# Three phases per batch in place of two, in a windowed-attention and gated-MLP kernel

## The chip, the cores and the metric

The kernel runs on one core of a Trainium2 chip. The metric is the device time of one execution in microseconds (us), the median of several runs. The "span" of a profile is the time from first to last instruction of the one profiled execution; it is about 1.7 to 2 us shorter than the timed value. Engines: PE is TensorE's matmul, PEld its weight load, DVE is VectorE, ACT is ScalarE, POOL is GpSimd, SP issues the output transfers.

## The reference, cut to what matters

Eight batches. Each has windowed attention (8 heads, 576 positions, width 64: four heads with a plain window of 32, four with a window dilated by 4), and then a gated MLP with a mixing matrix over the positions.

```python
scores = q @ k.T / sqrt(64)                  # masked by window, per head
attn   = softmax(scores);  x = concat_heads(attn @ v)        # (576, 512)
h = gelu_tanh(x @ w_in);  u, v = split(h)                    # (576, 512) each
v_n = (v - mean(v)) / sqrt(var(v) + 1e-6) * g_ln
v_s = w_sg @ v_n + b_sg                                      # over positions
out = x + (u * v_s) @ w_out
```

## The kernel before

The program is a list of small work items, each of which issues instructions to several engines. `merge` interleaves up to three lists. Every engine then works through its own instructions in the order of issue, so the interleaving fixes each engine's queue. The items of one batch `b`:

```python
a_T(b, g)    # transposes of q, k of a head pair: PE -> PSUM; copies qT, kT by ACT, half of kT by DVE (L223)
a_S(b, h)    # scores of a head: PE; exp by ACT; mask by DVE, or by POOL where h % 4 == 3
a_AV(b, g)   # value sums of a head pair: PE; DVE: reciprocal rc, then
             #     onorm = poa * rc        (L272, the eviction)
a_X(b, g)    # transpose of onorm: PE (pxt, L288); copy to xT by ACT (L291, or L295 and L297)
m_zv(b, i)   # v half of x @ w_in: PE (pz, L312); gelu by ACT (vv, L316); statistics st, mv by DVE (L321);
             #     rs = (var + 1e-6) ** -0.5 by POOL
m_vn(b, i)   # normalised v: DVE (vn, L331)
m_zu(b, ph)  # u half: PE (pu, L341); gelu by ACT
m_sgu(b, ph) # w_sg product: PE (pv, L354); DVE: vs = pv*g + b (L358), gat = u * vs (L361)
m_out(b, i)  # output product: PE (po, L371, L374); copy osb by ACT (L377); output by SP
```

PSUM has room for four of the tiles (`bufs=4`), taken in turn. The interleaving and the two phases of a period `p`:

```python
def merge(*lists):                      # every item of a list weighs the same
    items = [((i + 0.5) / len(x), n, i, f) for n, x in enumerate(lists)
             for i, f in enumerate(x)]
    for _, _, _, (f, *a) in sorted(items, key=lambda t: t[:3]):
        f(*a)

for p in range(B + 2):
    # first phase: T and S of batch p, beside sgu and out of batch p-2   (prep_wsg at p == 1)
    att = [T0, T1, S0, S1, T2, S2, S3, T3, S4, S5, S6, S7, cp_vd]       # (shortened)
    mlp = [sgu 0..3, out 0..2]                                          # (shortened)
    merge(att, mlp, io)
    # second phase: AV and X of batch p, beside zv, vn, zu of batch p-1
    att = [AV0, AV1, X0, AV2, X1, AV3, X2, X3]                          # (shortened)
    mlp = [zv0, zv1, vn0, zv2, vn1, zu0, vn2, zu1, zu2, zu3]            # (shortened)
    io  = [plain q, k of batch p+2; dilated q, k of batch p+2]          # (shortened)
    merge(att, mlp, io)
```

The softmax here doesn't subtract the row's maximum and nothing guards it: scores larger than these inputs give would overflow.

Of the kernel before, what the change touches and what calls it, by code (L numbers as in the profile page):

```python
# [11 lines left out]
FP16 = mybir.dt.float16  # L12
# [3 lines left out]
B, H, S, D = 8, 8, 576, 64  # L16
# [11 lines left out]
HS = S // 2  # L28
# [25 lines left out]
def kernel(  # L54
# [12 lines left out]
    nc = tc.nc  # L67
# [6 lines left out]
    sb = ctx.enter_context(tc.tile_pool(name="sb", bufs=2))  # L74
# [3 lines left out]
    def psum(name):  # L78
        return ps.tile([128, 2, 512], FP32, tag="ps", name=name)
# [25 lines left out]
    def setup_consts():  # L105
        nc.sync.dma_start(ident16, IDT.ap())
        nc.sync.dma_start(masks, MSK.ap())
        nc.vector.memset(mhalf, -0.5)
        for i in range(NKT):
            for hd in range(2):  # L110
                nc.vector.memset(kTs[i][hd], 0.0)
            nc.vector.memset(kIs[i], 0.0)
        for t in vps + vds:
            nc.vector.memset(t[0:HALO], 0.0)
            nc.vector.memset(t[:, :, :, 64:65], 1.0)
        for t in PTb:
            nc.vector.memset(t[:, S:PTW], 1.0)
        nc.vector.memset(wsgT16[0:64, 4, :], 0.0)


    def dma(dst, src):
        nc.gpsimd.dma_start(dst, src)  # L122
# [3 lines left out]
    def open_batch(b):  # L126
        qp = ld.tile([QB, NB, 4, D], FP16, tag="qp", name="qp")
        kp = ld.tile([QB, NB, 4, D], FP16, tag="kp", name="kp")
        qd = ld.tile([TB, 4, 2, 4, D], FP16, tag="qd", name="qd")
        kd = ld.tile([TB, 4, 2, 4, D], FP16, tag="kd", name="kd")  # L130
        loaded[b] = ((qp, kp), (qd, kd))

    def ld_plain(b, h0):
        if h0 == 0:
            open_batch(b)
        for t, src in zip(loaded[b][0], (q, k)):
            for h in range(h0, h0 + 2):
                dma(t[:, :, h, :], src[b][h].rearrange("(a p) d -> p a d", p=QB))

    def ld_dil(b):  # L140
        for t, src in zip(loaded[b][1], (q, k)):
            dma(t.rearrange("p h f r d -> p (h f) (r d)"),
                src[b][4:8].rearrange("h (f p r) d -> p (h f) (r d)", p=TB, r=4))

    def ld_vp(b, h0, n):
        vp = vps[b % NV]
        x = v[b][h0:h0 + n].rearrange("h (a p) d -> p (h a) d", p=QB)
        y = vp[:, h0:h0 + n].rearrange("p h a d -> p (h a) d")
        dma(y[HALO:KB, :, 0:D], x)
        dma(y[0:HALO, 1:, 0:D], x[QB - HALO:QB, 0:n * NB - 1])  # L150
# [3 lines left out]
    def ld_vd(b):  # L154
        vm = ld.tile([KB, 4, 4, D], FP16, tag="vm", name="vm")
        vt = ld.tile([KB, 4, 3, D], FP16, tag="vt", name="vt")
        x = v[b][4:8].rearrange("h (m r) d -> m h (r d)", r=4)
        dma(vm.rearrange("p h r d -> p h (r d)"), x[0:KB])
        for r in range(2):
            dma(vt[r:KB:2].rearrange("p h r d -> p h (r d)"),  # L160
                x[NM - 64:NM, :, D * r:D * r + 3 * D])
        vraw[b] = (vm, vt)
# [7 lines left out]
    def ld_win():  # L170
        dma(w_in16, moe_w_in.rearrange("(g p) f -> p g f", p=128))
# [25 lines left out]
    def a_T(b, g):  # L197
        plain, dil = loaded[b]
        pq, pk = psum("pq"), psum("pk")
        for t, pt in zip(plain if g < 2 else dil, (pq, pk)):  # L200
            if g < 2:
                for a in range(NB):
                    nc.tensor.matmul(pt[:, a // 3, QB * (a % 3):QB * (a % 3) + QB],
                                     t[:, a, 2 * g:2 * g + 2, :], ident16[0:QB, 0:QB],
                                     start=True, stop=True)
            else:
                for hd in range(2):
                    for c in range(4):
                        j, f = divmod(c, 2)
                        nc.tensor.matmul(pt[:, hd, TB * c:TB * c + TB],  # L210
                                         t[:, 2 * g - 4 + hd, f, 2 * j:2 * j + 2, :],
                                         ident16[0:TB, 0:TB], start=True, stop=True)
        qT = sb.tile([128, 2, HS], FP16, tag="qT", name="qT", bufs=3)
        nc.scalar.copy(qT, pq[:, :, 0:HS])  # L214
        if g < 2:
            kT = kTs[(2 * b + g) % NKT]
            k0, k1 = (kT[hd][64 * hd:64 * hd + 64, HALO:].rearrange(
                "p (j w) -> p j w", j=2) for hd in range(2))
        else:
            kT = kIs[(2 * b + g) % NKT]  # L220
            k0, k1 = (kT[64 * r:64 * r + 64, :, :, r] for r in range(2))
        nc.scalar.copy(k0, pk[0:64, :, 0:HS])
        nc.vector.tensor_copy(k1, pk[64:128, :, 0:HS])  # L223
        qkT[b, g] = (qT, kT)

    def a_S(b, h):
        qT, kT = qkT[b, h // 2]
        pss = psum("pss")
        if h < 4:
            kx, qx = kT[h % 2], qT.rearrange("p j w -> p (j w)")  # L230
            for a in range(NB):
                nc.tensor.matmul(pss[:, a // 3, QB * (a % 3):QB * (a % 3) + QB],
                                 kx[:, QB * a:QB * a + KB], qx[:, QB * a:QB * a + QB],
                                 start=True, stop=True)
        else:
            for j in range(2):
                kx = kT[:, h % 2, NM * j:NM * j + NM, :]
                qx = qT[:, h % 2, NM * j:NM * j + NM]
                for r in range(2):
                    nc.tensor.matmul(pss[:, j, 128 * r:128 * r + 128],  # L240
                                     kx[:, 0:KB, r], qx[:, 0:128], start=True, stop=True)
                nc.tensor.matmul(pss[:, j, 256:HS], kx[:, NM - 64:NM, :],
                                 qx[:, 128:NM].unsqueeze(1).broadcast_to([128, 2, 16]),
                                 start=True, stop=True)
        PT = PTb[(8 * b + h) % NPT]
        nc.scalar.activation(PT[:, 0:S].rearrange("p (j w) -> p j w", j=2),  # L246
                             pss[:, :, 0:HS], AF.Exp, scale=0.125)
        eng = nc.gpsimd if h % 4 == 3 else nc.vector
        eng.tensor_tensor(PT[:, 0:S], PT[:, 0:S], masks[:, h // 4], AO.mult)
        PTs[b, h] = PT  # L250

# [128 lines left out]
            nc.sync.dma_start(out[b][MT[ti] + lo:MT[ti] + 128, :], osb[lo:128, c, :])  # L380


    def merge(*lists):

        items = [((i + 0.5) / len(x), n, i, f) for n, x in enumerate(lists)
                 for i, f in enumerate(x)]
        for _, _, _, (f, *a) in sorted(items, key=lambda t: t[:3]):
            f(*a)

    setup_consts()  # L390
    for h0 in (0, 2):
        ld_plain(0, h0)
    ld_vp(0, 0, 4)
    ld_dil(0)
    ld_vd(0)
    ld_win()
    for p in range(B + 2):
        att, mlp, io = [], [], []
        if p < B:
            att = [(a_T, p, 0), (a_T, p, 1), (a_S, p, 0), (a_S, p, 1),  # L400
                   (a_T, p, 2), (a_S, p, 2), (a_S, p, 3),
                   (a_T, p, 3), (a_S, p, 4), (a_S, p, 5),
                   (a_S, p, 6), (a_S, p, 7), (cp_vd, p)]
        if p == 1:
            mlp = [(prep_wsg, i) for i in range(5)]
        if p >= 2:
            mlp = ([(m_sgu, p - 2, ph) for ph in range(4)] +
                   [(m_out, p - 2, i) for i in range(3)])
        if p + 1 < B:
            if p == 0:  # L410
                io = [(ld_plain, 1, 0), (ld_plain, 1, 2), (ld_dil, 1)]
            io += [(ld_vp, p + 1, 0, 4), (ld_vd, p + 1)]
        if p == 0:
            io += [(ld_wsg,)]
        if p == 1:
            io += [(ld_wout,)]
        merge(att, mlp, io)
        att, mlp, io = [], [], []
        if p < B:
            att = [(a_AV, p, 0), (a_AV, p, 1), (a_X, p, 0), (a_AV, p, 2), (a_X, p, 1),  # L420
                   (a_AV, p, 3), (a_X, p, 2), (a_X, p, 3)]
        if 1 <= p <= B:
            mlp = [(m_zv, p - 1, 0), (m_zv, p - 1, 1), (m_vn, p - 1, 0), (m_zv, p - 1, 2),
                   (m_vn, p - 1, 1), (m_zu, p - 1, 0), (m_vn, p - 1, 2)]
            mlp += [(m_zu, p - 1, ph) for ph in range(1, 4)]
        if p + 2 < B:
            io = [(ld_plain, p + 2, 0), (ld_plain, p + 2, 2), (ld_dil, p + 2)]
        merge(att, mlp, io)


# [28 lines left out]
```

## Time and profile before

| | before |
|---|---|
| time, median of the first 3 runs | 318.75 us |
| span of the profiled execution | 316.6 us |
| time from one batch's first pz to the next one's, undisturbed | 34.9 us |
| first pv (the fill) | 71.1 us |
| from the seventh batch's first pv to the end (the drain) | 37.2 us |

The profile page's first part (busy time and share of the span, by engine), and the first line of its fourth part (the chain of work that ended last, by engine):

```profile
PE 233.4 (74%) x2494; PEld 164.5 (52%) x2494; DVE 200.2 (63%) x378; ACT 185.3 (59%) x270; POOL 140.7 (44%) x191
...
DVE 35%; PE 29%; POOL 13%; ACT 10%; DMA 7%; issue 5%; POOLq 0%; DVEq 0%; ACTq 0%
```

No engine is near full, and the chain hops between all of them. The windows view splits one period into its two phases (second phase first). Columns: the stretch, its length, then busy time of PE, PEld, DVE, ACT and POOL with counts of instructions, the granted PE clock (1.00 is full speed), the time of the DMA packets as a share of the 16 DMA engines' time (above 1 where packets overlap), and GB/s:

```profile
123.70:141.00 17.30, 12.42 (x138) 8.34 (x136) 13.08 (x26) 10.89 (x17) 11.29 (x16) 1.00 0.57 68
141.00:158.60 17.60, 15.04 (x173) 10.88 (x173) 11.01 (x17) 12.47 (x20) 6.13 (x8) 1.00 1.03 119
```

In the first row PE works 12.4 of 17.3 us. The waits view says what it waits for (who waits and for what, with lines; then us in total, times, longest):

```profile
PE pxt L288 <- DVE onorm L272: 32.3, 23, 1.9
...
DVE st L321 <- ACT vv L316: 16.0, 8, 7.9
...
PE po L371 <- DVE gat L361: 8.6, 8, 1.1
```

The timeline of one second phase shows where the largest of these comes from. The brackets at the end of a line give the idle time before it and what ended it:

```profile
158.48 1.89 PE L312 MATMUL pz<-w_in_71,xT 128*128 128x512 f16 x8
...
165.01 0.43 PE L288 MATMUL pxt<-ident_69,onorm 96*128 96x96 f16 x6 [1.87 <-DVE onorm L272]
...
170.81 0.44 PE L288 MATMUL pxt<-ident_69,onorm 128*128 128x128 f16 x6 [1.28 <-DVE onorm L272]
...
173.87 0.66 PE L288 MATMUL pxt<-ident_69,onorm 128*128 128x128 f16 x6 [1.64 <-DVE onorm L272]
...
164.00 0.95 DVE L272 TENSOR_TENSOR onorm<-poa,rc 96x768 f16<-96x768 f32 x1
...
172.86 0.96 DVE L272 TENSOR_TENSOR onorm<-poa,rc 128x768 f16<-128x768 f32 x1
```

The phase opens with a zv group (pz at 158.48), and the first onorm starts at 164.00. The last starts at 172.86. Each X waits for its onorm, and PE cannot pass it.

### The profile page before, as it was taken

Reading aid. Unit: us, or ns where it says so; the run is one execution under the profiler, and the core shown is the slowest. Engines: PE = TensorE matmul, PEld = TensorE weight load, DVE = VectorE, ACT = ScalarE, POOL = GpSimd, SP = SyncE. Lnnn points to the kernel's source line nnn. Section 1 sums busy time; section 2 is a strip of 40 time slices with the busy share of each in tenths; the row PEclk is TensorE's granted clock in tenths of the full one; section 3 lists DMA queues with packets and bytes.
Section 4 is the critical chain, followed back from the end, with each engine's and each line's share of the span. In section 5 each row is a group of like instructions: output and inputs, shape, how many; then the busy total and the mean of one; then the engine's idle time right before and its main releaser. Section 6 shows DMA issues by size and latency. Waiting matters only on the chain.

```text
span 316.6 us, 6153 instructions
## 1 busy us (share of the span) xinstructions
PE 233.4 (74%) x2494; PEld 164.5 (52%) x2494; DVE 200.2 (63%) x378; ACT 185.3 (59%) x270; POOL 140.7 (44%) x191
## 2 busy tenths in 40 slices
PE   0373548868877779768876979768877878788984
PEld 0263445546545656546544756456545755564552
DVE  7533339957669493949478393949488665961760
ACT  1461549558475858477565858467666857533603
POOL 8946958492427741493229541593222011300400
PEclk9999999979999999999999899999999999999999
DMA  9999999699535997099626987099620004002104
GB/s 131 127 202 129 172 134 152 94 76 124 91 118 39 93 90 188 4 76 124 127 83 42 116 66 185 7 75 121 124 85 2 2 2 149 2 0 113 39 0 149
DMA packets 91467, 28.92 MB, mean 91 GB/s; under 512 B 71664, under 2 KB 86064, under 8 KB 91440
## 3 DMA queue, kind: packets, MB, share of 16 engines
q0 software_dynamic: 85232, 18.48, 66.2%
q1 hardware_dynamic: 6208, 10.06, 9.2%
q8 instruction: 19, 0.31, 0.4%
q14 instruction: 8, 0.07, 0.1%
HBM read 37.54 MB, written 9.44 MB: 148 GB/s over the span
## 4 chain that ended last, share of the span: by engine, by line
DVE 35%; PE 29%; POOL 13%; ACT 10%; DMA 7%; issue 5%; POOLq 0%; DVEq 0%; ACTq 0%
PE po L371 10%; DVE st L321 7%; DVE vs L358 6%; DVE onorm L272 5%; DVE gat L361 5%; PE pz L312 4%; DMA w_in_71<-in_moe_w_in_dram 4%; POOL kp L122 3%; PE pv L354 3%; PE po L374 3%; DVE vn L331 3%; DMA wsg_73<-in_moe_w_sg_dram 3%; ACT vv L316 3%; POOL rs L324 3%; POOL qp L122 2%
## 5 line engine op out<-in xcount | busy, mean ns | idle before, releaser
L371 PE MATMUL po<-w_out_72,gat 128*128 128x512 f16 x160 | 42.7, 379 | 8.6 <-DVE gat L361 8.6
L354 PE MATMUL pv<-wsgT_74,vn 128*128 128x288 f16 x320 | 43.9, 286 | 5.4 <-DVE kI_86 L223 1.2
L377 ACT COPY osb<-po 128x1024 f32<-128x1024 f32 (+1 forms) x24 | 21.0, 875 | 36.8 <-PE po L374 29.2
L288 PE MATMUL pxt<-ident_69,onorm 96*128 96x96 f16 (+2 forms) x192 | 15.3, 220 | 32.8 <-DVE onorm L272 32.3
L354 PEld LDWEIGHTS <-vn 128*128 128x128 f16 x320 | 30.8, 97 | 14.6 <-issue 5.6
L312 PE MATMUL pz<-w_in_71,xT 128*128 128x512 f16 x160 | 38.1, 379 | 0.2 <-ACT PT_95 L246 0.2
L341 PE MATMUL pu<-xT,w_in_71 128*128 128x288 f16 x256 | 37.9, 295 | 0.0
L321 DVE BATCH_NORM_STATS2 st<-vv 128x6 f32<-128x512 f32 x40 | 27.0, 675 | 16.0 <-ACT vv L316 16.0
L214 ACT CAST qT<-pq 128x576 f16<-128x576 f32 x32 | 20.5, 641 | 25.9 <-PE pq L210 13.0
L323 POOL TENSOR_SCALAR rs<-mv 128x2 f32<-128x2 f32 (+1 forms) x24 | 6.8, 282 | 59.9 <-DVE mv L322 59.5
L288 PEld LDWEIGHTS <-onorm 96*128 96x128 f16 (+1 forms) x192 | 10.6, 104 | 40.3 <-DVE onorm L272 40.3
L272 DVE TENSOR_TENSOR onorm<-poa,rc 96x768 f16<-96x768 f32 (+1 forms) x32 | 30.6, 956 | 1.1
L295 ACT CAST xT<-pxt 128x512 f16<-128x512 f32 x16 | 20.8, 1300 | 17.3 <-PE pxt L288 17.2
L344 ACT ACTIVATE u<-pu 128x576 f16<-128x576 f32 x32 | 21.9, 683 | 12.4 <-PE pu L341 12.4
L358 DVE SCALAR_TENSOR_TENSOR vs<-pv,g_col,b_bc 128x576 f16<-128x576 f32 x32 | 26.1, 814 | 4.3 <-PE pv L354 3.8
L122 POOL DMA_DIRECT2D kp<-in_k_dram x32 | 23.2, 728 | 9.2 <-DMA w_in_71<-in_moe_w_in_dram 3.9
L341 PEld LDWEIGHTS <-w_in_71 128*128 128x128 f16 x256 | 23.9, 100 | 6.0
L316 ACT ACTIVATE vv<-pz 128x1024 f32<-128x1024 f32 (+1 forms) x24 | 21.0, 881 | 9.0 <-PE pz L312 7.5
L122 POOL DMA_DIRECT2D qp<-in_q_dram x32 | 25.3, 797 | 1.5 <-POOLq L443 0.9
L371 PEld LDWEIGHTS <-gat 128*128 128x128 f16 x160 | 13.5, 97 | 21.4 <-DVE gat L361 13.7
L331 DVE TENSOR_SCALAR vn<-vv,mv,rs 128x512 f16<-128x512 f32 x40 | 21.3, 570 | 2.8 <-POOL rs L324 2.8
L312 PEld LDWEIGHTS <-xT 128*128 128x128 f16 x160 | 14.6, 98 | 14.0 <-issue 0.3
(179 smaller groups left out, 494.2 us busy)
## 6 DMA issues: line engine op xcount, KB each, us to landing
out_dram<-osb SPq DMA_DIRECT2D x32, 256.0 KB, 2.2
qp<-in_q_dram POOLq DMA_DIRECT2D x32, 72.0 KB, 3.0
kp<-in_k_dram POOLq DMA_DIRECT2D x32, 72.0 KB, 3.3
qd<-in_q_dram POOLq DMA_DIRECT2D x8, 288.0 KB, 6.1
kd<-in_k_dram POOLq DMA_DIRECT2D x8, 288.0 KB, 7.1
vm<-in_v_dram POOLq DMA_DIRECT2D x8, 256.0 KB, 4.4
vt<-in_v_dram POOLq DMA_DIRECT2D x16, 96.0 KB, 4.1
vp_87<-in_v_dram POOLq DMA_DIRECT2D x4, 288.0 KB, 8.5
```

Of the source, the lines that this page charges most:

```text
L122: nc.gpsimd.dma_start(dst, src)
L272: nc.vector.tensor_tensor(onorm.rearrange("p a h d -> p h a d"), pv[:, :, :, 0:64], rc.unsqueeze(3).broadcast_to([rows, 2, NB, 64]), AO.mult)
L288: nc.tensor.matmul(pxt[:, s // 3, c:c + n], onorm[:, s, :, :], ident16[0:rows, 0:n], start=True, stop=True)
L312: nc.tensor.matmul(pz[:, c, :], xT[:, g4, MT[ti]:MT[ti] + 128], w_in16[:, g4, DH:DFF], start=(g4 == 0), stop=(g4 == 3))
L316: nc.scalar.activation(vv[:, 0:n], pz[:, 0:n], AF.Gelu_apprx_tanh)
L321: nc.vector.bn_stats(st[:, c, :], vv[:, c, :])
L331: nc.vector.tensor_scalar(vn[:, ti, :], vv[:, c, :], mv[:, c, 0:1], rs[:, c, :], AO.subtract, AO.mult)
L341: nc.tensor.matmul(pu[:, j, 0:HS], w_in16[:, g4, 128 * ph:128 * ph + 128], xT[:, g4, HS * j:HS * j + HS], start=(g4 == 0), stop=(g4 == 3))
L344: nc.scalar.activation(us[b][:, ph, :].rearrange("p (j w) -> p j w", j=2), pu[:, :, 0:HS], AF.Gelu_apprx_tanh)
L354: nc.tensor.matmul(pv[:, j, 0:HS], vn[:, kp, 128 * ph:128 * ph + 128], wsgT16[:, kp, HS * j:HS * j + HS], start=(kp == 0), stop=(kp == 4))
L358: nc.vector.scalar_tensor_tensor(vs.rearrange("p (j w) -> p j w", j=2), pv[:, :, 0:HS], g_col[:, ph:ph + 1], b_bc.rearrange("p (j w) -> p ...
L371: nc.tensor.matmul(po[:, c, :], gat[:, ph, ts], w_out16[:, ph, :], start=(ph == 0), stop=False)
```

## The change

Three things: scores beside the gating unit, value sums beside the output product, and the first MLP half beside the next batch's transposes, with the MLP one period closer to its attention. The diff also brings two things: `merge` now weighs each item by an estimated cost, and the start-up is rearranged (w_sg is loaded ahead of batch 1's values, batch 0's dilated q and k ahead of its values, and batch 0's masks all go to VectorE). Besides, qT gets five buffers in place of three.

```diff
-        qT = sb.tile([128, 2, HS], FP16, tag="qT", name="qT", bufs=3)
+        qT = sb.tile([128, 2, HS], FP16, tag="qT", name="qT", bufs=5)
-        eng = nc.gpsimd if h % 4 == 3 else nc.vector
+        eng = nc.gpsimd if b and h % 4 == 3 else nc.vector
+    COST = {a_T: 0.7, a_S: 0.35, a_AV: 0.7, a_X: 0.4, m_zv: 1.5, m_zu: 1.0, m_sgu: 1.25,
+            m_out: 1.9, prep_wsg: 0.35}
     def merge(*lists):
-        items = [((i + 0.5) / len(x), n, i, f) for n, x in enumerate(lists)
-                 for i, f in enumerate(x)]
+        items = []
+        for n, x in enumerate(lists):
+            costs = [COST.get(f[0], 0.02) for f in x]
+            at = 0.0
+            for i, (f, c) in enumerate(zip(x, costs)):
+                items.append(((at + c / 2) / sum(costs), n, i, f))
+                at += c
...
-    for p in range(B + 2):
+    merge(T(0, range(4)))
+    for p in range(B + 1):
         # first phase
+            att = [(a_S, p, h) for h in range(8)] + [(cp_vd, p)]
+            mlp = [(m_sgu, p - 1, ph) for ph in range(4)]
+            io = [(ld_plain, 1, 0), (ld_plain, 1, 2), (ld_dil, 1), (ld_wsg,)]     # p == 0
         # second phase
             att = [AV0, AV1, X0, AV2, X1, AV3, X2, X3]                            # (shortened)
+            mlp = [(m_out, p - 1, i) for i in range(3)]
+            io = [(ld_vp, 1, 0, 4), (ld_vd, 1), (ld_wout,)]                       # p == 0
         # third phase
+            att = T(p + 1, range(4))
+            mlp = [zv0, zv1, vn0, zv2, vn1, zu0, vn2, zu1, zu2, zu3 of batch p]   # (shortened)
+            io = [(prep_wsg, i) for i in range(5)]                                # p == 0
```

More of the change, by code (lines that the diff above doesn't have):

```diff
@@ L380, in m_out, with T @@
             nc.sync.dma_start(out[b][MT[ti] + lo:MT[ti] + 128, :], osb[lo:128, c, :])
+    COST = {a_T: 0.7, a_S: 0.35, a_AV: 0.7, a_X: 0.4, m_zv: 1.5, m_zu: 1.0, m_sgu: 1.25,
+            m_out: 1.9, prep_wsg: 0.35}
     def merge(*lists):
-        items = [((i + 0.5) / len(x), n, i, f) for n, x in enumerate(lists)
-                 for i, f in enumerate(x)]
+        items = []
[5 more added lines that the diff above has]
+                at += c
         for _, _, _, (f, *a) in sorted(items, key=lambda t: t[:3]):
             f(*a)
+    def T(b, gs):
+        return [(a_T, b, g) for g in gs] if b < B else []
     setup_consts()
@@ L392 @@
         ld_plain(0, h0)
+    ld_dil(0)
     ld_vp(0, 0, 4)
-    ld_dil(0)
     ld_vd(0)
     ld_win()
-    for p in range(B + 2):
+    merge(T(0, range(4)))
+    for p in range(B + 1):
         att, mlp, io = [], [], []
         if p < B:
-            att = [(a_T, p, 0), (a_T, p, 1), (a_S, p, 0), (a_S, p, 1),
-                   (a_T, p, 2), (a_S, p, 2), (a_S, p, 3),
-                   (a_T, p, 3), (a_S, p, 4), (a_S, p, 5),
-                   (a_S, p, 6), (a_S, p, 7), (cp_vd, p)]
-        if p == 1:
-            mlp = [(prep_wsg, i) for i in range(5)]
-        if p >= 2:
-            mlp = ([(m_sgu, p - 2, ph) for ph in range(4)] +
-                   [(m_out, p - 2, i) for i in range(3)])
-        if p + 1 < B:
-            if p == 0:
-                io = [(ld_plain, 1, 0), (ld_plain, 1, 2), (ld_dil, 1)]
-            io += [(ld_vp, p + 1, 0, 4), (ld_vd, p + 1)]
+            att = [(a_S, p, h) for h in range(8)] + [(cp_vd, p)]
+        if p >= 1:
+            mlp = [(m_sgu, p - 1, ph) for ph in range(4)]
         if p == 0:
-            io += [(ld_wsg,)]
-        if p == 1:
-            io += [(ld_wout,)]
+            io = [(ld_plain, 1, 0), (ld_plain, 1, 2), (ld_dil, 1), (ld_wsg,)]
+        elif p + 1 < B:
+            io = [(ld_plain, p + 1, 0), (ld_plain, p + 1, 2)]
         merge(att, mlp, io)
@@ L421 @@
                    (a_AV, p, 3), (a_X, p, 2), (a_X, p, 3)]
-        if 1 <= p <= B:
-            mlp = [(m_zv, p - 1, 0), (m_zv, p - 1, 1), (m_vn, p - 1, 0), (m_zv, p - 1, 2),
-                   (m_vn, p - 1, 1), (m_zu, p - 1, 0), (m_vn, p - 1, 2)]
-            mlp += [(m_zu, p - 1, ph) for ph in range(1, 4)]
-        if p + 2 < B:
-            io = [(ld_plain, p + 2, 0), (ld_plain, p + 2, 2), (ld_dil, p + 2)]
-        merge(att, mlp, io)
+        if p >= 1:
+            mlp = [(m_out, p - 1, i) for i in range(3)]
+        if p == 0:
+            io = [(ld_vp, 1, 0, 4), (ld_vd, 1), (ld_wout,)]
+        elif p + 1 < B:
+            io = [(ld_dil, p + 1)]
+        merge(att, mlp, io)
+        if p < B:
+            att = T(p + 1, range(4))
+            mlp = [(m_zv, p, 0), (m_zv, p, 1), (m_vn, p, 0), (m_zv, p, 2),
+                   (m_vn, p, 1), (m_zu, p, 0), (m_vn, p, 2)]
+            mlp += [(m_zu, p, ph) for ph in range(1, 4)]
+            io = []
+            if p == 0:
+                io += [(prep_wsg, i) for i in range(5)]
+            elif p + 1 < B:
+                io += [(ld_vp, p + 1, 0, 4), (ld_vd, p + 1)]
+            merge(att, mlp, io)
 _INS = ['q', 'k', 'v', 'moe_w_in', 'moe_g_ln', 'moe_w_sg', 'moe_b_sg', 'moe_w_out']
```

## The prediction

> **What bounds it now.** No single engine. By the windows view one batch takes a period of 34.9 us (the same pz matmul recurs in the chain of waits at 88.8, 123.7, 158.6, 194.7, 229.6, 263.7). A period holds 27.4 us of TensorE, 24.1 of VectorE, 23.4 of ScalarE; the rest is waits inside in-order queues (chain: VectorE 35%, TensorE 29%, GpSimd 13%, ScalarE 10%). In the second phase VectorE is fullest (13.1 of 17.3 us): four onorm evictions (0.96 us) share its queue with five st (0.68) and five vn, and TensorE waits 32 us in all for onorm (waits view). The rs pair on GpSimd sits among ten q/k DMA issues (0.75 us each). Around the periods are a fill of 53 us (DMA about 99% busy in the slices; w_sg lands at 43.6) and a drain from 279.5 to 316.6.
>
> **What the change does.** No arithmetic is removed. It
> 1. removes one stage of depth: the drain step "sgu + out of batch 6" (279.5 to 291, 11.5 us) moves into a full period, batch 0's first MLP half into the fill;
> 2. asks for w_sg before batch 1's values (0.83 MB less ahead of it at 150 GB/s: 5 us earlier, estimate 38), and keeps batch 0's masks off GpSimd, which hold AV until 35 us now;
> 3. spreads GpSimd: rs shares a phase with 5 DMA issues, not 10;
> 4. takes st and vn out of the phase with onorm;
> 5. adds a tight chain: zv directly follows X of the same batch. The last xT copies (1.30 + 0.40 us, twice) come first on ScalarE; estimated 2.5 us of idle TensorE per period. Table loads (1.28 us) go from 13 to 16.
>
> **A period, costed** from timeline durations. Scores + sgu: TensorE 7.1, VectorE about 9.5, ScalarE 5.6. AV + X + out: 8.4, 4.5, 6.2. Transposes + zv + zu: 10.3, 9.8, 10.5. The maxima add to 28.4, against 27.8 for the two phases now: a tie by work alone. Walking the queues by hand (four PSUM tiles, in order) gives 4.5 us from the last AV to zv, 12.6 for phase three, 16.1 for phases one and two: 33.2; with unmodelled gaps I take 34. The steady state gains only about 1 us per batch.
>
> **Sum.** Batch 0's third phase ends at about 52.5 us; six periods of 34 = 204; phases one and two of batch 7, 20.6; zv + zu, 9.5; the last sgu + out, 15.6 as now. 302 us of span, 303 timed. Most of the gain is fill and drain; about 6 us is the period. Break-even is a period near 36.5.
>
> **What the profile would show.** First pz of each batch 33 to 35 us apart; first pv at about 52 (71 now); TensorE waiting about 2 us for xT before each batch's first pz; VectorE light in the AV phase; GpSimd well under 13% of the chain; onorm waits much below 32 us; w_sg landing at 36 to 40.
>
> The Trainium skill's "Perfetto Trace Analysis" (Tensor Engine Instruction) calls ScalarE, VectorE and GpSimd strict FIFO. The trace agrees: ready work stands behind waiting copies (kT casts waiting 10.3 us). So interleaving order, not busy time, decides.
>
> **What would make it wrong.** Phase three limited by PSUM rotation (VectorE frees pk behind st and vn), or phase one by VectorE with the sgu chain exposed: a period over 35.5 removes the 2%. Eight loads issued beside the masks may delay PT 3 and 7. If phases overlap more than I walked, a period of 31 gives 285.

## The result, and the profile after

The time is 307.25 us (median of four runs, 305.54 to 308.69), against 318.97 us for the kernel before in the same rounds. The ratio is 0.9639, with a 95% interval of 0.9582 to 0.9696: faster by 3.6%. The ratios here and below are worked out from runs of the same rounds, so they are not quite the ratios of the medians.

The page's first part and the first line of the chain, after:

```profile
PE 237.3 (78%) x2494; PEld 165.0 (54%) x2494; DVE 196.2 (64%) x380; ACT 188.0 (62%) x272; POOL 139.3 (46%) x189
...
DVE 3%; PE 3%; ACT 1%; POOLq 0%; issue 0%; POOL 0%; DVEq 0%; ACTq 0%
```

The chain cannot be compared: in this trace it could be followed back only from the end to 278 us, so its shares add up to 8% of the span. The windows view of one period, third phase first, then first and second:

```profile
140.44:155.35 14.91, 11.44 (x112) 7.28 (x110) 8.24 (x17) 12.89 (x20) 5.50 (x9) 1.00 0.56 78
155.35:163.37 8.02, 7.36 (x90) 6.09 (x88) 6.54 (x13) 6.25 (x10) 7.40 (x11) 1.00 1.05 94
163.37:175.36 11.99, 10.23 (x114) 6.87 (x112) 8.36 (x15) 4.29 (x6) 4.56 (x5) 0.86 0.95 128
```

The waits view after:

```profile
DVE st L321 <- ACT vv L316: 55.3, 9, 6.7
...
PE po L371 <- DVE gat L361: 12.8, 8, 1.8
...
PE pz L312 <- ACT xT L295: 11.8, 14, 0.9
...
PE pxt L288 <- DVE onorm L272: 2.8, 3, 1.7
```

The wait for onorm is gone (32.3 us to 2.8). In its place PE waits 11.8 us for xT, which it never did before, and 12.8 us instead of 8.6 for gat; and VectorE, which used to be the fullest engine of its phase, now waits 55.3 us for the first vv of each batch. The timeline shows both waits, in two different batches:

```profile
98.11 0.39 PE L371 MATMUL po<-w_out_72,gat 128*128 128x512 f16 x1 [1.76 <-DVE gat L361]
...
98.67 1.91 PE L371 MATMUL po<-w_out_72,gat 128*128 128x512 f16 x4
...
140.44 0.59 PE L312 MATMUL pz<-w_in_71,xT 128*128 128x512 f16 x2
141.83 0.39 PE L312 MATMUL pz<-w_in_71,xT 128*128 128x512 f16 x1 [0.81 <-ACT xT L295]
...
143.11 1.25 PE L312 MATMUL pz<-w_in_71,xT 128*128 128x512 f16 x5 [0.89 <-ACT xT L295]
```

The second line is a group of four matmuls that takes 1.91 us; the same group takes 1.03 us in other batches. That is a drop of the PE clock: the trace's clock records have it at half speed for 3.41 us from 98.4, and again from 166.7 and 235.0 (the third row of the windows above holds the second drop, hence its 0.86). It comes in every second batch, so the period alternates between 33.4 and 34.9 us.

The 14 profiles together show when such a drop comes. In each profile the drops start whole multiples of 3.41 us apart, as on a fixed grid. Cut each profile into stretches of this grid, from 60 us to 8 us before the end and leaving out those already inside a drop: this gives 917 stretches. In 54 of them PE was busy for less than 54% of the time, and 26 of these were followed by a drop; of the other 863 none was. In the kernel after, PE was busy for 1.65 of the 3.41 us before each of its three drops (windows view). In the batch from 122.2 the same wait of 1.76 us (131.26 to 133.02) is split by the grid at 132.5 into stretches with 2.14 and 2.92 us of work, and no drop follows. So in these profiles every drop came behind a thin stretch, but a thin stretch was not enough: half of the 54 had no drop behind them.

**Where the time came from.** The first pv of each batch cuts a span into a fill (up to the first), six full periods, and a drain (from the seventh to the end). These numbers are worked out from the timelines of the profiled executions:

| | fill | mean of six periods | drain | fill + drain |
|---|---|---|---|---|
| before | 71.1 | 34.71 | 37.2 | 108.4 |
| after | 54.5 | 34.08 | 46.8 | 101.2 |

Of the 10.9 us of span, 7.2 come from fill and drain and 6 x 0.63 = 3.8 from the period (rounded). That is close to the prediction's split. The table also shows something the prediction did not expect: the fill is 16.7 us shorter, but the drain is 9.6 us longer. Whether the shallower pipeline itself brings anything is the first question for the experiments.

### The profile page after: what moved, and what is told of

Read it like the earlier page. It is cut to its first block, busy times and chain, and to the rows that moved or that the text cites. A ratio compares the mean times of both kernels' runs of the same rounds, so it can differ in the third digit from the quotient of the medians. Undisturbed runs are those within 1.5% of the kernel's fastest.

```text
span 305.7 us, 6136 instructions
## 1 busy us (share of the span) xinstructions
PE 237.3 (78%) x2494; PEld 165.0 (54%) x2494; DVE 196.2 (64%) x380; ACT 188.0 (62%) x272; POOL 139.3 (46%) x189
## 5 line engine op out<-in xcount | busy, mean ns | idle before, releaser
L321 DVE BATCH_NORM_STATS2 st<-vv 128x6 f32<-128x512 f32 x40 | 27.2, 679 | 55.7 <-ACT vv L316 55.3
L312 PE MATMUL pz<-w_in_71,xT 128*128 128x512 f16 x160 | 44.1, 404 | 18.1 <-ACT xT L295 11.8
L371 PE MATMUL po<-w_out_72,gat 128*128 128x512 f16 x160 | 45.4, 399 | 12.8 <-DVE gat L361 12.8
L354 PE MATMUL pv<-wsgT_74,vn 128*128 128x288 f16 x320 | 45.0, 286 | 6.2 <-DVE vn L331 1.8
L341 PE MATMUL pu<-xT,w_in_71 128*128 128x288 f16 x256 | 35.1, 286 | 3.2 <-ACT u L344 2.6
L354 PEld LDWEIGHTS <-vn 128*128 128x128 f16 x320 | 29.2, 97 | 15.4 <-issue 5.3
L341 PEld LDWEIGHTS <-w_in_71 128*128 128x128 f16 x256 | 24.9, 98 | 11.6 <-issue 4.7
L371 PEld LDWEIGHTS <-gat 128*128 128x128 f16 x160 | 14.4, 102 | 26.7 <-DVE gat L361 17.0
L214 ACT CAST qT<-pq 128x576 f16<-128x576 f32 x32 | 20.3, 634 | 13.1 <-PE pq L203 10.9
L344 ACT ACTIVATE u<-pu 128x576 f16<-128x576 f32 x32 | 20.9, 652 | 8.0 <-PE pu L341 7.9
L122 POOL DMA_DIRECT2D qp<-in_q_dram x32 | 24.2, 766 | 2.2 <-DMA kd<-in_k_dram 0.9
L361 DVE TENSOR_TENSOR gat<-u,vs 128x576 f16<-128x576 f16 x32 | 20.5, 642 | 1.4
L295 ACT CAST xT<-pxt 128x512 f16<-128x512 f32 x16 | 20.6, 1346 | 0.6 <-PE pxt L288 0.6
L324 POOL TENSOR_TENSOR rs<-rs,mhalf 128x2 f32<-128x2 f32 (+1 forms) x24 | 17.5, 729 | 2.0
```

Of the source, the lines that this page charges most:

```text
L122: nc.gpsimd.dma_start(dst, src)
L312: nc.tensor.matmul(pz[:, c, :], xT[:, g4, MT[ti]:MT[ti] + 128], w_in16[:, g4, DH:DFF], start=(g4 == 0), stop=(g4 == 3))
L321: nc.vector.bn_stats(st[:, c, :], vv[:, c, :])
L341: nc.tensor.matmul(pu[:, j, 0:HS], w_in16[:, g4, 128 * ph:128 * ph + 128], xT[:, g4, HS * j:HS * j + HS], start=(g4 == 0), stop=(g4 == 3))
L344: nc.scalar.activation(us[b][:, ph, :].rearrange("p (j w) -> p j w", j=2), pu[:, :, 0:HS], AF.Gelu_apprx_tanh)
L354: nc.tensor.matmul(pv[:, j, 0:HS], vn[:, kp, 128 * ph:128 * ph + 128], wsgT16[:, kp, HS * j:HS * j + HS], start=(kp == 0), stop=(kp == 4))
```

## The experiments

Theory A, the prediction's: the removed drain stage and the earlier start-up bring the fill and drain gain, the three phases bring about 1 us per period. Rival B: the depth is worth little. Rival C: the weights, which the prediction did not mention at all, carry the steady-state gain. Twelve kernels ran; all gave correct results. Period (the mean of the six) and fill + drain of a row below are from its own profile, and the time is a median of four runs beside the kernel before on the same chip (before: 318.9 to 319.8 us). e9, e10 and e11 ran on another chip than the rest.

| run | phases | weights | start-up | time, us | ratio to before | period | fill + drain |
|---|---|---|---|---|---|---|---|
| before | 2 | no | old | 319 | 1 | 34.71 | 108.4 |
| e3 | 2 | no | new | 314.4 | 0.984 | 34.74 | 104.0 |
| e4 | 2 | yes | old | 300.95 | 0.941 | 32.05 | 106.9 |
| e6 | 2 | yes | new | 292.45 | 0.919 | 31.80 | 101.1 |
| e5 | 3 | no | new | 314 | 0.989 | 34.24 | 102.9 |
| e2 | 3 | yes | old | 311.0 | 0.972 | 33.77 | 107.6 |
| after | 3 | yes | new | 307.25 | 0.964 | 34.08 | 101.2 |

### e1_deep3: three phases at the old depth

```diff
-    for p in range(B + 1):
+    for p in range(B + 2):
-            mlp = [(m_sgu, p - 1, ph) ...]      # and m_out, p - 1; m_zv, m_vn, m_zu, p
+            mlp = [(m_sgu, p - 2, ph) ...]      # and m_out, p - 2; m_zv, m_vn, m_zu, p - 1
```

prep_wsg moves to the first phase of p = 1.

> The three phases of the changed kernel, but with the old depth: the MLP of batch p-1 runs beside batch p+1's transposes, its sgu and output one period later. Theory A (my prediction: most of the gain is the removed drain stage, about 11.5 us): the period stays near 34.1 us or falls by the 1.7 us xT wait at most, but a drain stage comes back, so the time is clearly above the changed kernel's 307 us, about 312 to 318. Rival B (depth as such is worth little: the shallow version only moves batch 7's lone attention phases to the end, about 47 us of tail against about 38, and what gained is the fill and the phase grouping): the time is within 1.5% of 307 us, and the first pz no longer waits for xT.

Measured: 304.01 us, ratio 0.951. One period deeper is not slower but about 1% faster than the changed kernel. An undisturbed period is 32.2 us. Theory A asked for 312 us or more and falls; rival B holds. This run alone does not separate the depth from the wait for xT, because the deeper version also loses most of that wait (2.1 us in 5 waits, against 11.8 in 14). The cut by first pv does not fit e1, whose sixth period is short (26.8 us: no transposes of a next batch are left). Over the five periods before it e1 takes 165.7 us and the kernel after 169.5; the rest of the span is 137.4 us in e1 and 136.2 in the kernel after. By this cut the stage of depth is worth about 1 us at the ends, not 11.5; each clock drop, some 1.5 us, blurs it.

### e2_latefill and e3_beforefill: the start-up edits taken away, and alone

```diff
 # e2, on the kernel after                          # e3, on the kernel before: the reverse
-    eng = nc.gpsimd if b and h % 4 == 3 else nc.vector
+    eng = nc.gpsimd if h % 4 == 3 else nc.vector
-    ld_dil(0); ld_vp(0, 0, 4)
+    ld_vp(0, 0, 4); ld_dil(0)
-    io = [plain 1, dil 1, wsg]; second phase: [vp 1, vd 1, wout]
+    io = [plain 1, dil 1, vp 1, vd 1, wsg]; second phase: [wout]
```

> The changed kernel with the old load order (batch 1's values ahead of w_sg, batch 0's values ahead of its dilated q/k) and batch 0's h%4==3 masks back on GpSimd. If the fill is bound by the arrival of w_sg, the first pv moves from 54.5 to about 60 us and the whole time rises by about 5 us, to about 312, with an unchanged period of 34.1 us. If the fill is bound by something else, the time stays within 1% of 307.

> The kernel before with only the start-up edits: w_sg ahead of batch 1's values, dilated q/k ahead of values for batch 0, batch 0's masks all on VectorE. If the start-up edits alone are worth what I put on them (5 us), the time is about 314 us with an unchanged period of 34.9 us; if they are worth more than half of the 11.5 us gain, it is under 313; if nothing, 319.

Measured: 310.98 and 314.39 us. The tile view of pv (first and last start at the end of the line) gives the fill of before, after, e2, e3 and e6, in this order, one fence each:

```profile
L354 PE MATMUL pv<-wsgT_74,vn x320: 282/286/297, 71.1 to 305.3; 128*128 128x288 f16 x160
```

```profile
L354 PE MATMUL pv<-wsgT_74,vn x320: 282/286/297, 54.4 to 294.4; 128*128 128x288 f16 x160
```

```profile
L354 PE MATMUL pv<-wsgT,vn x320: 282/286/448, 59.3 to 299.0; 128*128 128x288 f16 x160
```

```profile
L354 PE MATMUL pv<-wsgT,vn x320: 282/286/338, 66.8 to 301.1; 128*128 128x288 f16 x160
```

```profile
L354 PE MATMUL pv<-wsgT,vn x320: 282/286/448, 63.9 to 280.6; 128*128 128x288 f16 x160
```

The start-up edits move the first pv by about 5 us in both kernels (59.3 to 54.4, and 71.1 to 66.8), and the time by about 4 to 5 us, as predicted. And e2 says what the rest of the change does at the ends: with the old start-up, the three-phase kernel's fill and drain are 107.6 us, against 108.4 for the two-phase kernel before (which also lacks the weights). The pair that differs in nothing but the third phase and its depth is e6 and after: 101.1 and 101.2 us. **The third phase with its shallower depth brings nothing measurable at the ends: what the fill loses (63.9 to 54.4), the drain gains (37.2 to 46.8).** With e1, which changes the depth alone, that leaves the removed stage no gain near 11.5 us. Work that ran without a partner at the start now runs without one at the end.

### e4_beforeweights and e7_weights_second: the weights alone, and only in the second phase

```diff
 # e4: the kernel before with the new merge and COST, nothing else
 # e7: the same, but in the first phase
-        merge(att, mlp, io)
+        merge(att, mlp, io, weighted=False)
```

> The kernel before with only the cost-weighted interleaving of its two phases. Rival C: the weights, not the three phases, bring the steady-state gain; then the period falls from 34.9 to about 34.1 us and the time to about 313. If the grouping matters, the period stays within 0.3 us of 34.9 and the time within 1% of 319.

> The kernel before with the weights in its second phase only (value sums beside the first MLP half). If the gain of the weights is that zv, st and vn no longer come before the onorms in VectorE's queue, all of it is here: period 31 to 31.6 us, about 300 us. If the first phase's order matters as much, the period is near 33 and the time near 310.

Measured: 300.95 us for e4 (ratio 0.941) and 300.77 us for e7. The weights alone, on two phases, bring more than the whole change and far more than the 6 us that were expected of them (313 us), and by the time all of it sits in the second phase (e7's undisturbed period is 32.2 us, against 31.6 for e4, so the first phase's order may be worth a little more per batch). The items of the second phase by the two rules (worked out from the program, loads left out):

```
equal:    zv0 AV0 zv1 AV1 vn0 X0  zv2 AV2 vn1 zu0 X1  vn2 AV3 zu1 X2  zu2 X3  zu3
weighted: AV0 zv0 AV1 zv1 vn0 X0  zv2 AV2 vn1 zu0 X1  vn2 zu1 AV3 zu2 X2  zu3 X3
```

In e4 the first onorm starts 1.0 us after the first pz (5.5 us before), the last one 12.1 us after it (14.4 before). Lines of e4's timeline for this phase, to be held against those of before:

```profile
151.02 1.89 PE L312 MATMUL pz<-w_in,xT 128*128 128x512 f16 x8
...
161.47 0.44 PE L288 MATMUL pxt<-ident,onorm 128*128 128x128 f16 x6 [0.93 <-DVE onorm L272]
...
164.13 0.66 PE L288 MATMUL pxt<-ident,onorm 128*128 128x128 f16 x6 [1.23 <-DVE onorm L272]
...
152.04 0.95 DVE L272 TENSOR_TENSOR onorm<-poa,rc 96x768 f16<-96x768 f32 x1
...
163.12 0.96 DVE L272 TENSOR_TENSOR onorm<-poa,rc 128x768 f16<-128x768 f32 x1
```

And its line of the waits view:

```profile
PE pxt L288 <- DVE onorm L272: 15.6, 16, 1.2
```

PE's wait for onorm is halved: it falls by 16.7 us (32.3 to 15.6), about as much as the span (17.4 us: 316.6 less 299.2). In the weighted order the value sums AV0 and AV1 each stand ahead of zv0 and zv1, so that onorm enters VectorE's queue before st, and X2 and X3 each have one more zu group ahead of them, which PE can do while VectorE works off st, vn and onorm.

### e9_av0_first: one move only

```diff
-            att = [(a_AV, p, 0), (a_AV, p, 1), ...
+            a_AV(p, 0)
+            att = [(lambda: None,), (a_AV, p, 1), ...
```

> The kernel before with one move: in the second phase the first value sum (AV of head pair 0) is issued ahead of the first zv group, all else where it was. The weights move the same pair and also shift zv, vn and zu by a place or two. If what the weights gained is that the onorm chain starts before st enters VectorE's queue, this one move gives most of it: period 31.6 to 32.5 us, time 300 to 305. If the gain needs the spreading of zv and zu as well, the period stays above 33.8 and the time above 312.

Measured: 312.44 us, ratio 0.980 with a 95% interval of 0.973 to 0.987 (the verdict at 2% is unclear, but it is faster). The undisturbed period is 33.75 us. The first onorm now starts 2.0 us after the first pz, and the last 12.7 us after it (14.4 before, 12.1 in e4). So the early AV0 alone is about a third of the weights' gain in the undisturbed period (1.15 of 3.3 us); the rest needs the other shifts (AV1 ahead of zv1, AV3 and X2, X3 behind zu). Which of those matters most was not separated.

### e5_three_uniform: three phases without weights

```diff
-            costs = [COST.get(f[0], 0.02) for f in x]
+            costs = [1.0 for f in x]
```

> The changed kernel with every item of a phase weighing the same (the interleaving rule of before). With the runs so far this completes the square of two or three phases, old or new weights. If the weights help three phases as they helped two (3.2 us of period), the time rises from 307 to about 330. If three phases in themselves already do what the weights do for two (onorm no longer shares its phase with st and vn), it stays within 1% of 307.

Measured: 313.98 us with a wide scatter (310.1 to 317.3; ratio 0.989, interval 0.977 to 1.002, unclear). The run of 317.3 is slow; the three fast ones (310.1, 313.5, 314.4) have a mean of 312.7 us, against 319.2 for the four of before, 2.0% less. Neither expectation was met: the weights are worth some 5 to 7 us on three phases, against 18 to 22 on two. The period of the profiled execution, which is the fastest of the four, is 34.3 us, without a clock drop. This answers the square: the new grouping does remove the onorm waits (3.2 us in all), more fully than the weights (15.6), but PE then waits 19.3 us for gat and 9.6 for xT. With equal weights the period is 0.5 us shorter than with two phases (e3), though the time is the same (314.0 and 314.4); with weights the third phase costs 2.3 us of period (e6 31.80, after 34.08).

### e6_two_weights_fill: everything but the third phase

```diff
 # e3's start-up edits and e4's merge, on the kernel before
```

> The two-phase kernel with the weights and the start-up edits, and no third phase. If the two gains are independent, 319 less 5 (start-up) less 18 (weights): about 296 us, period 31.6 to 33, first pv at about 65. If the weights' gain already hides the start-up, about 301. Either way, below 307 it would show that the third phase, as built, costs time.

Measured: 292.45 us, ratio 0.919. That is better than the two gains alone add up to (about 296 us), and 14.8 us faster than the changed kernel. So the change as a sum, on the spans, in the order start-up, weights, third phase: -4.2 (before to e3), -20.5 (e3 to e6), +13.8 (e6 to after), together -10.9 us. In another order the shares differ (the weights on three phases bring at most 7 us, e5 to after), but in no pair that differs by it (e3 and e5, e4 and e2, e6 and after) does the third phase show a clear gain.

### e8_xt_dve and e11_three_xt_mask: two waits of the third phase

```diff
 # e8, on the kernel after, in a_X for g >= 2
-            nc.scalar.copy(x[...], pxt[...])                     # two copies
+            cp = nc.vector.tensor_copy if g == 3 else nc.scalar.copy
+            cp(x[...], pxt[...])
 # e11: e8, and all masks on VectorE
-        eng = nc.gpsimd if b and h % 4 == 3 else nc.vector
+        eng = nc.vector
```

> The changed kernel with the last of the four xT evictions moved from ScalarE to VectorE, which sits idle for 6.7 us there. If the chain from the last X to zv costs what the trace shows (TensorE waits 0.81 + 0.89 us for xT in each batch), the period falls by 1.2 to 1.7 us, to 32.4 to 32.9, and the time to 294 to 298. If that wait only hides another one (ScalarE's table load of 1.28 us before the first vv, or PSUM tiles), the period falls by under 0.5 us and the time stays above 303.

> The changed kernel with the last xT eviction on VectorE (298.6 us so far) and all masks on VectorE. This tests the second wait of three phases: TensorE stands 1.76 us before the output product of each batch for the last gat, which takes 1.09 us beside GpSimd's mask of PT 7 and 0.46 us without. If that collision is what it waits for, the wait falls to about 1.2 us and the time by 3 to 5 us, to about 294 to 296. If VectorE's queue of the phase sets it, moving two masks there lengthens it and the time stays at 298 or rises.

Measured: 298.6 us for e8 and 293.0 us for e11. The last xT copy off ScalarE takes 8.7 us off the time, and its undisturbed period is 32.4 against 33.4 us (some 6 us over six; most of the rest is one clock drop less): the chain X, xT, zv of one batch was on the bound. The wait for xT is about halved, and the longer wait of VectorE for vv shrinks with it. Lines of the waits view of e8, of which the last is the wait of 11.8 us in the kernel after:

```profile
DVE st L322 <- ACT vv L317: 31.9, 9, 3.7
...
PE po L372 <- DVE gat L362: 12.8, 8, 1.8
...
PE pz L313 <- ACT xT L296: 5.6, 7, 0.8
```

The masks on VectorE take another 5.6 us. PE's wait for the last gat falls, as this line of e11's timeline shows (1.76 us in the kernel after):

```profile
159.74 0.39 PE L372 MATMUL po<-w_out,gat 128*128 128x512 f16 x1 [1.34 <-DVE gat L362]
```

That is 0.4 us in this batch, and 2.5 us over the run (12.8 to 10.3 in the waits view). About 3 us more come from the clock: in e8 two of the six periods still had a drop and took 33.9 instead of 32.4 us, in e11 none has one and the last five are 31.8 to 31.9 us. e8 and e11 together bring the three phases level with the best two-phase kernel (293.0 and 292.45 us). So removing parts of these two waits wins back 14.3 us, about what the third phase cost (14.8). That they are the cost fits e6's trace, which has neither: PE never waits there for xT before pz, and all 32 gat take 0.46 us (in the kernel after, 14 of 32 overlap a mask of GpSimd and take 0.69 to 1.1). But the same two edits on two phases were not run, so it is not shown that they would bring nothing there, and "level" does not say that three phases are as good as two can be.

### e10_x3_late: a wait that only moved

```diff
 # on e6: X3 out of the second phase, behind T0 of the next first phase
+            att.insert(1, (a_X, p - 1, 3))
```

> The two-phase kernel with weights and start-up edits (292.5 us), with the last transposition X3 moved behind the first transposes of the next period's first phase. There TensorE waits 0.94 us (X2) and 1.24 us (X3) for onorm in each period, and in some periods a drop of the granted clock follows (the next pv group takes 2.56 instead of 1.39 us). If those waits lie on the bound, the period falls by 1.2 to 2.5 us and the time to 273 to 283. If VectorE or ScalarE bounds the period in their place, it stays above 288.

Measured: 296.43 us (ratio 0.928, interval 0.921 to 0.935), a miss: no gain, and by the medians about 4 us slower than e6. The two ran on different chips and the intervals of their ratios overlap (e6: 0.912 to 0.926), so the loss is less certain than the missing gain. PE no longer waits for X3, but X2 now waits longer, and the next pv waits for a PSUM tile that the late xT copy holds. From e10's timeline:

```profile
161.99 0.44 PE L288 MATMUL pxt<-ident,onorm 128*128 128x128 f16 x6 [1.79 <-DVE onorm L272]
...
163.94 1.39 PE L354 MATMUL pv<-wsgT,vn 128*128 128x288 f16 x10 [1.00 <-ACT xT L297]
```

The period alternates between 31.6 and 33.3 us, the longer ones with a clock drop (from 66.6, 131.4 and 196.3 us; e6 has a single one, from 158.3). Without a drop it is the 31.6 us of e6, so the place of X3 in PE's queue is not the bound. That VectorE's chain of onorms is the bound instead fits this, but is not shown.

### e12_three_best: an attempt at a version that beats both

```diff
 # on e11, at the start of the third phase
+            nc.scalar.activation(junk, mhalf, AF.Gelu_apprx_tanh)     # two columns, only to load the table
-            att = T(p + 1, range(4))
+            att = T(p + 1, range(1, 4))
+            a_T(p + 1, 0)                                              # if there is a batch p + 1
```

> Aimed at a version that beats both kernels and the 292.5 and 293 us of the runs so far. Three phases with the last xT on VectorE and all masks on VectorE (period 31.85 us), and two additions at the start of the third phase: a one-column gelu on ScalarE right after the last xT eviction, so that the 1.28 us table load runs while ScalarE waits for zv (the trace shows it idle 1.2 us there and loading after), and the first transposes of the next batch issued ahead of zv, into the 0.81 us that TensorE waits for xT. If the table load and the xT wait lie on the bound, the period falls by 1.0 to 1.6 us and the time to 281 to 286; if VectorE's st queue sets the phase, under 0.4 us a period and the time stays above 290.

Measured: 290.71 us, ratio 0.913: the fastest of all by its median, though only 0.6% below e6, and short of the 281 to 286 us that I had hoped for. The period falls by 0.4 us, to 31.45. In the ScalarE timeline the table load did move: it directly follows the last xT copy, and the copies of the next batch's qT and kT come after it. (In the kernel after it starts at 144.43, 1.24 us after the last xT copy ends and just after the first pz group ends at 144.36.)

```profile
136.81 0.41 ACT L299 CAST xT<-pxt 128x64 f16<-128x64 f32 x1
137.24 1.28 ACT L437 ACT_TABLE_LOAD   x1
138.53 0.20 ACT L437 ACTIVATE junk<-mhalf 128x2 f32<-128x2 f32 x1
```

But PE then waits for VectorE, which frees the PSUM tile of the k transposes late. Two lines of the PE timeline, and one of the waits view:

```profile
137.27 1.89 PE L314 MATMUL pz<-w_in,xT 128*128 128x512 f16 x8 [0.86 <-ACT xT L299]
...
140.63 2.75 PE L314 MATMUL pz<-w_in,xT 128*128 128x512 f16 x12 [0.91 <-DVE kT L224]
...
DVE kT L224 <- ACT kT L223: 18.1, 9, 2.5
```

That is a limit by the PSUM tiles, which the prediction named as a risk, but not by the path that it named (VectorE freeing pk behind st and vn). VectorE is idle for 2.46 us before this copy of kT (139.82 to 140.58): it waits for ScalarE's half of kT, which ends at 139.79, behind the early table load, the gelu on junk and the copy of qT. It became visible only once the waits in front of it were gone.

## Why the prediction was right, point by point

The prediction said 303 us; the time is 307.25 us. The number and the direction were right. The reason it gave for the larger part was not, and part of the agreement in the period is luck (point 1).

1. **The sum.** Its terms against the trace (us): first pv at 52.5, measured 54.5; six periods of 34, measured 34.08 on average; the lone phases one and two and zv + zu of batch 7, 20.6 + 9.5 = 30.1, measured 31.2 (258.93 to 290.09, from where the last pv no longer wait for vn; the first of them is at 287.06); the last sgu + out 15.6, measured 15.6. It sums to 302 against a span of 305.7. Walking the queues by hand, with durations from the trace, was good to about 1%. For the period this holds of the walk itself, 33.2 against the undisturbed 33.4; that the 34 with "unmodelled gaps" also meets the mean of 34.08 is luck, because what was added in the run are clock drops of 1.5 us in every second period, which the walk did not have.
2. **"Removes one stage of depth: ... (11.5 us)"**: this step failed as a cause. The stage does vanish from the drain, but the drain grows as much as the fill shrinks (e2 with before; e6 with after), and a deeper three-phase kernel is faster and loses only about 1 us at the ends (e1). What fill and drain gained in sum, 7.2 us, is mostly the start-up edits (4 to 6 us in the pairs before/e3 and e2/after).
3. **"w_sg landing at 36 to 40"**: right. The first transpose of w_sg ran at 38.1 us (43.7 before), and the start-up edits are worth about the 5 us that were put on them.
4. **"A tie by work alone ... the steady state gains only about 1 us per batch"**: right as a number (0.63 us), but incomplete. The prediction compared the three phases with the two phases *as they were interleaved before*, and never costed the new weights in `merge`. They alone take the two-phase period from 34.7 to 32.05 us (e4). The small gain per batch is a large gain from the weights (2.9 us, e3 to e6) less a large loss from the third phase (2.3 us, e6 to after). The prediction named neither, so the close number does not support its explanation.
5. **"Takes st and vn out of the phase with onorm"**: right as a mechanism; the wait for onorm fell from 32.3 to 2.8 us. But the weights, a smaller edit, remove half of it without a third phase.
6. **"A tight chain: ... estimated 2.5 us of idle TensorE per period"**: right in kind, but over-estimated: 1.7 us measured (0.81 + 0.89), and e8 shows that it is on the bound. Table loads went from 14 to 16 in all, two more and not three.
7. **"GpSimd well under 13% of the chain"**: not decided, because the chain of the new trace ends at 278 us.
8. **"Interleaving order, not busy time, decides"**: right in the sense that order alone moved the time most, and more than was meant. The prediction leaned on the Trainium skill's "Perfetto Trace Analysis" (section "Tensor Engine Instruction (MATMUL, LD_WEIGHTS)"), which calls ScalarE, VectorE and GpSimd strict FIFO. e4 and e9 agree: with the same instructions in another order, PE's wait for onorm goes from 32.3 to 15.6 us, and the time from 319 to 301 us. Having written that sentence, I should have costed the one edit in the diff that changes nothing but order.

Two things stay open. The clock drops come only after stretches of thin PE work, but not after all of them (every second batch of after, none in the full periods of the profiled e5 and e11), and no run here isolates what decides. And nobody ran e8's and e11's two edits on the two-phase kernel.

## What to carry to other kernels

When a diff restructures a pipeline and also changes how work is interleaved, cost the interleaving by itself first: here it was worth more than the restructuring, and an ablation of a few lines showed it. Making a pipeline shallower shortens the fill but can lengthen the drain by the same amount; count both ends. Before placing a consumer right behind its producer, look at which engine evicts between them, and move that eviction to the engine that is idle there.

## What the Trainium skill lacked or had wrong

- "ScalarE: Activation LUTs", section "What ACT_TABLE_LOAD costs", gives about 1283 ns for the load and about 1380 ns of drain, 2.66 us per switch. The load agrees (1.28 us). The drain does not show here: in e12 the load starts 0.02 us after the copy in front of it ends (136.81 + 0.41 to 137.24) and the activation starts 0.01 us after the load, so a switch costs 1.3 us; the gap in front of the load is 0.02 us for all 13 loads of the kernel before that have work ahead of them, too. The page also does not say that a small activation placed early pulls the load forward into idle time, as e12 shows.
- "TensorE: Matmul & The Clock Gate", section "What's actually happening", ties the fall to the half rate to an idle window of about 3.4 us. The half rate and the length agree (0.5 for 3.41 us; four matmuls took 1.91 instead of 1.03 us). But the window in front need not be idle: PE was busy for 1.65 of 3.41 us before each of the three drops of the kernel after, and for up to 53% before others; nor is it enough, as 28 of 54 such thin stretches had no drop behind them.
- "GPSIMD Engine Reference", section "1. Specifications", says that GpSimd shares its SBUF interfaces with VectorE and that instructions with two SBUF inputs contend. The trace agrees: gat (two SBUF inputs) takes 0.46 us alone and 1.09 us beside a GpSimd mask of 1.29 us. How long the wait lasts is not in this section (the skill goes into the sharing elsewhere): all 14 gat of the kernel after that overlap a mask end 0.31 to 0.33 us after the mask does, so by these traces gat waits for the whole mask.
- No page says how to interleave lists of unequal work items on in-order queues; here placing them by estimated cost in place of by count was worth 18 us of 319 (e4).
